# Attention followed by a gated long convolution on one core: another written order for the first two batches, and other transfers for the last rows

## The chip, the cores and the metric

The kernel runs on one core of a Trainium2 chip. The metric is the device time of one execution in microseconds (us). The runs shown of the kernel before have a median of 230.85 us (230.39 to 231.59).

## What is computed

The reference has two halves. A linear attention without softmax, normalised by head, gives `x`; then `x` is projected into three parts, one of them is convolved along the sequence with a filter given in time (576 points, by FFT), multiplied by the two others, and projected out. Batch 8, heads 8, sequence 576, head size 64, so a model size of 512.

```
kv   = einsum('bhsd,bhse->bhde', k, v)
out  = einsum('bhsd,bhde->bhse', q, kv)
attn = out / sqrt(mean(out*out, -1) + 1e-6) * g_norm
x    = attn as [B, S, 512]

x1, x2, x3 = split(x @ w_proj)
X2 = rfft(x2, axis=1);  H = rfft(filter, axis=0)
y  = x1 * irfft(X2 * H) * x3
result = y @ w_out
```

## The kernel before

Everything is written for one core with a schedule made by hand. The body is cut into small named steps, most of them one matmul group on PE (TensorE) or one eviction on ACT (ScalarE) or DVE (VectorE). Three word lists, `FIRST`, `ROUND` and `LAST`, name the steps in the order in which they are issued; a `+` behind a name means one batch later than the round's number, a `-` one batch earlier, and a step that has been issued is not issued again. `FIRST` runs once, `ROUND` for r = 0 to 6, `LAST` once. Each engine works through its own steps in this order, so the lists set the order on PE, ACT, DVE, POOL (GpSimd) and SP (SyncE) alike. Waits between engines follow from the data and the buffers.

The steps of one batch:

- `Lk`, `Lv`, `Lq` (line 98): loads of K, V and Q, 576 KB each in bf16 after a cast from f32, all issued from POOL into one queue, two buffers each (by the batch's parity). For batch 0 K and V come in halves (`Lka`, `Lkb`, `Lva`, `Lvb`). `Lf` loads the filter, `Lw1` to `Lw3` the three thirds of `w_proj`, `Lwo` the output weights.
- `Qt` (line 333): a DMA transpose of Q, issued from SP; batches 0 and 1 use PE instead (`T0`, `T1`, evicted by `eTv` on DVE or `eTa` on ACT).
- `K` (line 307): K transposed times V on PE; `eK` evicts it. For batch 0 in two halves, `Ka` and `Kb`.
- `O0` to `O3` (line 372): attention output for two heads each; `sq` squares it on ACT, `ob` (ACT) or `ov` (DVE, batch 0) scales it by `g_norm`; `R` sums the squares on PE, `rs` takes the reciprocal root on ACT; `x0` and `x1` (line 408, DVE) multiply to `x`.
- `fd`, `fr`, `fa` (DVE): folds of `x` for a transform split by three and by parity. `rrM`, `rrT`, `abM`, `abT` (PE): projection of the folds with the second third of `w_proj`; `err`, `eab`, `eT` (ACT) evict.
- `F0`, `F1`, `F2` (PE): forward transform. `M0`, `M1`, `M2` (DVE): products with the filter's spectrum; `A0` (POOL) and `Av1` (DVE) add them up.
- `Ga0` to `Ga3` and `Gb0` to `Gb3` (line 531, PE): the first and third part of the projection; `x10` to `x13` (ACT) and `g0` to `g3` (DVE) evict and multiply them.
- `Io`, `I` (PE), `os` (ACT), `u`, `w`, `fin` (DVE): inverse transform, unfolding, gate product into `yg`.
- `U0`, `U2`, `U4` (PE, lines 604 and 618): output projection; `ot0`, `ot2`, `ot4` (ACT) evict it and issue the stores, four each, from SP. The last batch uses `V0` to `V3` (one chunk of 128 rows each) with `va` on ACT or `vv` on DVE. `ot_tile` (line 600) hands out three output buffers in turn.

Steps that run once: `Z`, `Zi`, `Zt`, `Zf` (constants), `An0` to `An2` (sine and cosine tables), `Act` (loads ACT's function table for the reciprocal root), `Tb0` to `Tb2` (transposed tables), `Ff0` to `Ff2` (folded filter), `H0` to `H2` (line 269, the filter's spectrum). A step `W..._` adds four matmuls (the first of them ten) without use for the result ahead of the next PE step that takes a PSUM pair (line 78): they keep PE busy.

PSUM is held as four pairs of two banks. A step that writes PSUM takes the pair that was freed longest ago in the written order (line 74), and waits for the step that frees it.

Of the kernel before, what the change touches and what calls it, by code (L numbers as in the profile page):

```python
# [23 lines left out]
Lk++ R1+ x1+ Ga3 Ga2 g1 Io01 rs1+ Gb3 x13 Lv++ x0+ fr+ x12 os01 I01 rrM+ rrT+ fd+ fa+ g3 err+ abT+ eT+ Io23
u01 os23 I23 abM+ F0+ eab+ Gb2 F2+ u23 M0+ F1+ g2 M1+ w23 fin23 w01 fin01 K++ Lk+++ Qt++ Lq+++ eK++ W12_ O2++"""

ROUND = """K++ Lk+++ x0+ Qt++ U0- Lq+++ x13 eK++ fd+ Io23 u01 O2++ fa+ Gb3 fr+ ot0- Lv+++ os23 I23 abM+ g3 sq2++ u23
ob2++ rrM+ eab+ abT+ rrT+ eT+ U4- O1++ w01 err+ ot4- sq1++ ob1++ O3++ sq3++ fin01 ob3++ F1+ U2- w23 fin23 F0+
ot2- M1+ Ga1+ x11+ F2+ Ga0+ M0+ Gb0+ x10+ A0+ R3++ M2+ O0++ Gb1+ g0+ R2++ rs3++ Ga2+ g1+ sq0++ Av1+ ob0++
rs2++ R0++ x1++ Gb2+ x12+ R1++ rs0++ rs1++ g2+ Ga3+ Io01+ os01+ I01+"""  # L30

LAST = """u01 Io23 x13 U0- I23 w01 U2- os23 u23 fin01 ot0- Gb3 w23 ot2- g3 fin23 V2 V1 U4 va2 vv1 V3 V0 ot4 vv3 va0"""


@with_exitstack
def kernel(
# [232 lines left out]
    def gen_h(g):  # L269
        ff = tmp['ff']  # L270
        hp = take("h")
        n = N1 if g == 0 else P
        for ri in range(2):
            for a in range(3):
                m = P if a < 2 else 32
                kw = dict(start=(a == 0), stop=(a == 2))
                if g < 2:
                    nc.tensor.matmul(hp[:n, ri], FW[:m, a, 2 * g + ri, 0:n], ff[:m, a, ri], **kw)
                else:
                    for dup in range(2):  # L280
                        nc.tensor.matmul(hp[dup * NM:(dup + 1) * NM, ri], FW[:m, a, 4 + ri, ri * NM:(ri + 1) * NM], ff[:m, a, ri], **kw)
        u = work.tile([P, 2, DM], FP32, name="hu", tag="ot%d" % g)
        if g < 2:
            todo = [(HH[:n, g, 1], 0, cf[:n, 0, g:g + 1], cf[:n, 1, g:g + 1]),
                    (HH[:n, g, 0], 1, cf[:n, 0, g:g + 1], cf[:n, 2, g:g + 1])]
        else:
            todo = [(HM[:, i], 0, pc[:, 2 * i:2 * i + 1], pc[:, 2 * i + 1:2 * i + 2]) for i in range(2)]
        for i, (o_, ri, c1, c2) in enumerate(todo):
            act.activation(out=u[:n, i], in_=hp[:n, ri], func=AF.Copy, scale=c1)
            vec.scalar_tensor_tensor(out=o_, in0=hp[:n, 1 - ri], scalar=c2, in1=u[:n, i], op0=ALU.mult, op1=ALU.add)  # L290
# [307 lines left out]
    turn = [0]  # L598

    def ot_tile():  # L600
        turn[0] += 1
        return buf("ot", turn[0] % 3, [P, 2, DM], FP32)

# [5 lines left out]
                nc.tensor.matmul(pp[:, cc], ygt(b)[:, dc, c * P:(c + 1) * P], wo[:, dc], start=(dc == 0), stop=(dc == NDC - 1))  # L609

    def U_ev(b, c0):
        ot = ot_tile()
        act.copy(out=ot, in_=tmp['u', b, c0])  # L613
        free(("u", b, c0))
        for i in range(4):
            nc.sync.dma_start(out=o_rows(b, 4 * c0 + i, 4 * c0 + 4 + i), in_=ot[32 * i:32 * i + 32])
# [5 lines left out]
                nc.tensor.matmul(pp[64 * i:64 * i + 64], ygt(b - 1 + i)[:, dc, 4 * P:S], wo[:, dc], start=(dc == 0), stop=(dc == NDC - 1))  # L622

    def U4_ev(b):
        ot = ot_tile()
        act.copy(out=ot[:, 0], in_=tmp['u4', b])
        free(("u4", b))
        for i in range(4):
            nc.sync.dma_start(out=o_rows(b - 1 + i // 2, NB - 2 + i % 2), in_=ot[32 * i:32 * i + 32, 0])

    for c0 in (0, 2):
        step["U%d" % c0] = lambda b, c0=c0: U(b, c0)
# [7 lines left out]
        for dc in range(NDC):  # L640
            nc.tensor.matmul(pp, ygt(b)[:, dc, c * P:(c + 1) * P], wo[:, dc], start=(dc == 0), stop=(dc == NDC - 1))

    def V_ev(b, c, ev, q1):
# [1 line left out]
        ev(out=ot[:, 0], in_=tmp['u', b, c])
        free(("u", b, c))
        for i in range(4):
            (q1 if i >= 2 else nc.sync).dma_start(out=o_rows(b, 4 * c + i), in_=ot[32 * i:32 * i + 32, 0])
# [60 lines left out]
```

## Time and profile before

| what | us |
|---|---|
| median of the runs shown | 230.85 |
| the profiled execution | 231.38 |
| its span on the core | 229.6 |
| PE busy | 209.0 |
| DVE busy | 191.7 |
| ACT busy | 152.3 |

The span is what the profile's times count from and to; the time of the same execution has 1.8 us around it. An engine's busy time counts its own instructions, and matmul ends are modelled, so a busy PE isn't PE at its peak. In a row of the timeline the first number is the start, the second the duration; in brackets stands how long the engine was idle ahead of it and what ended that. A group's row gives, behind the bar, the busy time, the mean of one instruction in ns, and the idle time ahead of them.

### The profile page before, as it was taken

How to read it: one execution, taken by the hardware profiler on the slowest of the kernel's cores; microseconds unless marked ns; L12 is line 12 of the kernel's file. 1: busy time of each engine (PE TensorE's matmuls, PEld its weight loads, DVE VectorE, ACT ScalarE, POOL GpSimd, SP SyncE). 2: the span in 40 equal slices, each digit the busy share in tenths (PEclk: the TensorE clock that was granted, in tenths of full speed). 3: DMA queues.
4: the chain of work that ended last, by engine and by line, in shares of the span. 5: the costliest groups of instructions: out<-in, count | busy, mean ns of one | idle time of the engine just before them, and what ended most of it. 6: DMA issues, size and time to landing. Idle time of an engine off the chain costs nothing.

```text
span 229.6 us, 4731 instructions
## 1 busy us (share of the span) xinstructions
PE 209.0 (91%) x1860; PEld 126.4 (55%) x1881; DVE 191.7 (83%) x323; ACT 152.3 (66%) x238; POOL 45.8 (20%) x55
## 2 busy tenths in 40 slices
PE   7397897899989999999999999999999999999770
PEld 2244433476547755775577557745774676467320
DVE  4864587789898999899889998998899989998920
ACT  7737866995468768776877688768776784533421
POOL 7751000550080000800080008000400040012030
PEclk9859999999999999999999999999999999999995
DMA  4999998599969630999299919993803120350464
GB/s 44 195 202 205 204 207 138 103 142 204 192 100 199 98 91 18 185 184 213 62 185 175 224 34 174 188 206 79 162 3 91 41 55 21 87 126 0 114 179 121
DMA packets 41193, 30.14 MB, mean 131 GB/s; under 512 B 16050, under 2 KB 36530, under 8 KB 41170
## 3 DMA queue, kind: packets, MB, share of 16 engines
q0 software_dynamic: 21200, 17.11, 49.3%
q1 hardware_dynamic: 19778, 12.46, 24.0%
q8 instruction: 15, 0.25, 0.4%
q10 hardware_dynamic: 192, 0.26, 0.4%
q14 instruction: 8, 0.07, 0.1%
HBM read 33.69 MB, written 9.44 MB: 188 GB/s over the span
## 4 chain that ended last, share of the span: by engine, by line
PE 72%; DVE 15%; ACT 6%; issue 2%; DMA 2%; POOL 1%; ACTq 0%; DVEq 0%; POOLq 0%
PE ps L537 26%; PE ps L609 9%; PE ps L464 5%; PE ps L561 4%; PE ps L383 3%; PE ps L471 3%; PE ps L450 3%; PE ps L313 2%; PE ps L376 2%; PE ps L261 2%; PE ps L505 2%; PE ps L497 2%; DMA out_dram<-ot 2%; PE ps L457 1%; PE ps L490 1%
## 5 line engine op out<-in xcount | busy, mean ns | idle before, releaser
L537 PE MATMUL ps<-x,wp 128*128 128x288 bf16 x512 | 71.3, 286 | 0.6 <-ACT o L393 0.5
L537 PEld LDWEIGHTS <-wp 128*128 128x128 bf16 x512 | 49.0, 98 | 17.1 <-issue 1.1
L518 POOL TENSOR_TENSOR Y<-tpw 97x1024 bf16<-97x1024 f32 x8 | 18.8, 2353 | 157.8 <-PE ps L537 79.3
L475 ACT CAST x<-ps 128x1024 bf16<-128x1024 f32 (+1 forms) x24 | 20.3, 871 | 16.3 <-PE ps L464 8.9
L543 ACT CAST x<-ps 128x576 bf16<-128x576 f32 x32 | 20.5, 644 | 12.5 <-PE ps L537 12.0
L545 DVE TENSOR_TENSOR g<-ps,x 128x576 bf16<-128x576 f32 x32 | 24.0, 754 | 5.3 <-PE ps L537 5.1
L609 PE MATMUL ps<-wo,yg 128*128 128x512 bf16 x105 | 26.1, 380 | 0.4
L397 ACT ACTIVATE rstd<-ps,bias_eps 128x576 bf16<-128x576 f32 x32 | 23.6, 745 | 4.2 <-PE ps L383 3.3
L386 ACT ACTIVATE sq<-ps 128x576 bf16<-128x576 f32 x32 | 21.0, 662 | 1.7 <-PE ps L376 1.7
L511 DVE TENSOR_TENSOR tpw<-ps,HH 97x1024 f32<-97x1024 f32 (+1 forms) x16 | 19.5, 1220 | 2.0 <-PE ps L498 1.3
L393 ACT ACTIVATE o<-ps,g_col 128x576 bf16<-128x576 f32 x28 | 21.1, 758 | 0.0
L512 DVE TENSOR_TENSOR tpw<-ps,HH 97x1024 f32<-97x1024 f32 (+1 forms) x16 | 19.4, 1215 | 0.0
L613 ACT COPY ot<-ps 128x1024 f32<-128x1024 f32 x14 | 14.3, 1022 | 7.5 <-PE ps L609 7.4
L609 PEld LDWEIGHTS <-yg 128*128 128x128 bf16 x112 | 10.4, 98 | 11.6
L561 PE MATMUL ps<-IV,Y 128*128 128x192 bf16 x128 | 16.2, 245 | 0.0
L464 PE MATMUL ps<-wp,ab 128*128 128x512 bf16 x64 | 15.1, 379 | 0.0
L565 ACT COPY os<-ps 128x576 f32<-128x576 f32 x16 | 10.3, 642 | 7.1 <-PE ps L562 6.1
L383 PE MATMUL ps<-sq,ind 128*128 128x288 bf16 x64 | 12.9, 286 | 1.9 <-ACT sq L386 1.6
L570 DVE TENSOR_TENSOR u<-ps,os 128x576 bf16<-128x576 f32 x16 | 12.0, 750 | 1.8 <-ACT os L565 1.8
L409 DVE TENSOR_TENSOR x<-o,rstd 128x1152 bf16<-128x1152 bf16 x16 | 12.1, 755 | 1.4 <-ACT rstd L397 1.3
L562 PE MATMUL ps<-IV,Y 97*128 97x96 bf16 x64 | 13.2, 207 | 0.0
L79 PE MATMUL ps<-kvblk,ind 128*128 128x512 bf16 x35 | 11.5, 452 | 1.8 <-DVE ind L145 1.6
(137 smaller groups left out, 339.0 us busy)
## 6 DMA issues: line engine op xcount, KB each, us to landing
out_dram<-ot SPq DMA_DIRECT2D x56, 128.0 KB, 2.4
qb<-in_q_dram POOLq DMA_DIRECT2D x8, 576.0 KB, 9.7
kb<-in_k_dram POOLq DMA_DIRECT2D x7, 576.0 KB, 7.1
vb<-in_v_dram POOLq DMA_DIRECT2D x7, 576.0 KB, 11.7
...
```

The costliest lines, as they stand in the source:

```text
L383: nc.tensor.matmul(r2[:, h, 0:TH], ind, sq()[:, j, h * TH:(h + 1) * TH], start=True, stop=True)
L386: act.activation(out=halves(sq()[:, j]), in_=tmp['o', b, j][:, :, 0:TH], func=AF.Square)
L393: act.activation(out=by_time(osb(), j), in_=i_, func=AF.Copy, scale=g_col)
L397: act.activation(out=by_time(rstd(), j), in_=by_row(tmp['r', b, j]), func=AF.Abs_reciprocal_sqrt, scale=1.0 / D, bias=bias_eps)
L464: nc.tensor.matmul(pp[:, h], abt()[:, j, h * SB:h * SB + P], w2(j), start=(j == 0), stop=(j == NDC - 1))
L475: act.copy(out=o_(), in_=tmp[key, b])
L511: vec.tensor_mul(out=t_[:n, 0], in0=xp[:n], in1=HH[:n, g, 1:3])
L537: nc.tensor.matmul(pp[:, h, 0:TH], w_, x[:, j, h * TH:(h + 1) * TH], start=(j == 0), stop=(j == NDC - 1))
L543: act.copy(out=x1, in_=pp[:, :, 0:TH])
L545: vec.tensor_mul(out=halves(g13t()[:, dc]), in0=pp[:, :, 0:TH], in1=x1)
L561: nc.tensor.matmul(pp[:, i, 0:SB], Y[:, 2 * g + h, cs], IV[:, 2 * g + h, 0:SB], start=(g == 1), stop=(g == 2))
L609: nc.tensor.matmul(pp[:, cc], ygt(b)[:, dc, c * P:(c + 1) * P], wo[:, dc], start=(dc == 0), stop=(dc == NDC - 1))
```

## The change

Three things change.

First, `FIRST` is written anew and is longer: it now reaches to step `I23` of batch 1, and `ROUND` begins at another point of the cycle and has another order inside. For the engines this means:

- Loads are written as Q, then K and V of batch 0 in halves, the filter, Q of batch 1, two thirds of `w_proj`, K of batch 1, the last third, V of batch 1, K, V and Q of batch 2, `w_out`. Before, the filter stood second and the loads of K and V of batch 2 stood behind `A0` of batch 0 on POOL.
- `Act` stands after the sine tables instead of ahead of them.
- The warm-up steps `W6_` to `W9_` and `W12_` are gone; `W0_`, `W1_` and `W2_` stay.
- `Ga0`, `Ga1` of batch 0 stand ahead of K of batch 1, and so on.
- A load into a buffer that a DMA transpose still reads (`Lq++++` after `Qt++`) is written behind the transpose, and in the rounds `Lk`, `Qt`, `A0`, `Lv`, `Lq` follow one another on POOL and SP in another order.

Second, `gen_h` (steps `H0` to `H2`) issues its ACT copies ahead of both DVE products, for g = 0 and 1 as one instruction over both banks.

Third, the last rows. For the last two batches every second output tile is laid into `sq`, `o` or `rstd`, which nothing uses any more, so that six buffers take turns. Two chunks of the last batch share a tile and leave in four transfers of 128 KB (`vd0`, `vd2`, from SP), where each chunk had four of 64 KB from SP and from ACT or POOL. The four transfers of the last `ot4` go from POOL. The order of `LAST` follows.

```diff
-FIRST = """Z Lq Lf Zi Lka Act Zt Lva An0 An1 An2 Lvb W0_ T1 Zf T0 eTv0 eTv1 Tb0 Lkb Lq+ Lw2 Ff2 Ff0 Tb2 Ff1 W2_ Ka eKa W1_ Tb1 O1 sq1
...
+FIRST = """Z Lq Zi W0_ Lvb Zt An0 T1 An2 T0 An1 Lkb Zf eTv0 eTv1 Lka Act W2_ Tb2 Kb eKb Lva Lf Tb1 O3 O2 Ka W1_ sq3 sq2
+eKa R2 R3 Lq+ Lw1 ov2 rs2 ov3 O1 O0 rs3 sq0 ov0 sq1 ov1 Tb0 Lw2 Ff1 Ff0 x1 Lk+ Ff2 R1 R0 Lw3 T1+ rs1 T0+ rs0
+x0 fr0 fr1 eTa1+ eTa0+ H1 fd1 Ga0 Ga1 rrM fa1 x10 x11 fd0 fa0 H2 rrT err H0 abM F0 Lv+ K+ abT Lk++ eK+ O0+ eT
+Lv++ eab Lq++ M0 Gb1 sq0+ ob0+ F1 O1+ sq1+ g1 R0+ Ga3 rs0+ ob1+ M1 F2 O3+ x13 O2+ sq3+ Qt++ sq2+ M2 Av1 ob3+
+Gb3 Lwo Gb0 ob2+ A0 R1+ R2+ g3 R3+ Lq++++ rs1+ g0 x0+ rs2+ rs3+ K++ Io23 x1+ Ga2 eK++ fr+ Io01 x12 O3++ fd+
...
+ROUND = """fd+ fa+ ot0- Ga3 fr+ os23 x13 O2++ I23 sq2++ ob2++ Gb3 abM+ rrM+ g3 abT+ u23 w01 eab+ eT+ rrT+ U4- O1++ O3++
+err+ w23 F1+ ot4- U2- Lk+++ sq1++ sq3++ Qt+++ ob1++ ob3++ F0+ ot2- Ga0+ R3++ fin01 M1+ Ga1+ x10+ rs3++ F2+ M0+
+R1++ A0+ x11+ rs1++ R2++ rs2++ Gb0+ Gb1+ O0++ Av1+ sq0++ M2+ Ga2+ g0+ fin23 ob0++ x12+ Gb2+ Lv++++ Lq+++++
+R0++ g1+ K+++ x1++ Io01+ g2+ I01+ rs0++ U0 os01+ x0++ eK+++ Io23+ u01+"""
-LAST = """u01 Io23 x13 U0- I23 w01 U2- os23 u23 fin01 ot0- Gb3 w23 ot2- g3 fin23 V2 V1 U4 va2 vv1 V3 V0 ot4 vv3 va0"""
+LAST = """I23 w01 os23 u23 Ga3 ot0- fin01 x13 Gb3 w23 U2- ot2- g3 fin23 U4 V3 V2 vv3 ot4 V1 vv1 va2 vd2 V0 va0 vd0"""

+        if g < 2:
+            act.activation(out=u[:n], in_=hp[:n], func=AF.Copy, scale=todo[0][2])
+        else:
+            for i in range(2):
+                act.activation(out=u[:n, i], in_=hp[:n, 0], func=AF.Copy, scale=todo[i][2])
         for i, (o_, ri, c1, c2) in enumerate(todo):
-            act.activation(out=u[:n, i], in_=hp[:n, ri], func=AF.Copy, scale=c1)
             vec.scalar_tensor_tensor(out=o_, in0=hp[:n, 1 - ri], scalar=c2, in1=u[:n, i], op0=ALU.mult, op1=ALU.add)

-    def ot_tile():
+    def ot_tile(b):
+        if b >= B - 2:
+            turn[1] += 1
+            if turn[1] % 2:
+                t = (sq, osb, rstd)[turn[1] // 2 % 3]()
+                return t.rearrange("p a b -> p (a b)").bitcast(FP32)[:, 0:2 * DM].rearrange("p (a b) -> p a b", a=2)
         turn[0] += 1
         return buf("ot", turn[0] % 3, [P, 2, DM], FP32)

-            nc.sync.dma_start(out=o_rows(b - 1 + i // 2, NB - 2 + i % 2), in_=ot[32 * i:32 * i + 32, 0])
+            (nc.gpsimd if b == B - 1 else nc.sync).dma_start(out=o_rows(b - 1 + i // 2, NB - 2 + i % 2), in_=ot[32 * i:32 * i + 32, 0])

-    def V_ev(b, c, ev, q1):
-        ot = ot_tile()
-        ev(out=ot[:, 0], in_=tmp['u', b, c])
+    def V_ev(b, c, ev):
+        if c // 2 not in tmp:
+            tmp[c // 2] = ot_tile(b)
+        ev(out=tmp[c // 2][:, c % 2], in_=tmp['u', b, c])
         free(("u", b, c))
-        for i in range(4):
-            (q1 if i >= 2 else nc.sync).dma_start(out=o_rows(b, 4 * c + i), in_=ot[32 * i:32 * i + 32, 0])
+
+    def V_out(b, c0):
+        for i in range(4):
+            nc.sync.dma_start(out=o_rows(b, 4 * c0 + i, 4 * c0 + 4 + i), in_=tmp[c0 // 2][32 * i:32 * i + 32])
```

More of the change, by code (lines that the diff above doesn't have):

```diff
@@ L24 @@
[L24 to L29, printed above, removed]
@@ new lines @@
+Lv++ eab Lq++ M0 Gb1 sq0+ ob0+ F1 O1+ sq1+ g1 R0+ Ga3 rs0+ ob1+ M1 F2 O3+ x13 O2+ sq3+ Qt++ sq2+ M2 Av1 ob3+
+Gb3 Lwo Gb0 ob2+ A0 R1+ R2+ g3 R3+ Lq++++ rs1+ g0 x0+ rs2+ rs3+ K++ Io23 x1+ Ga2 eK++ fr+ Io01 x12 O3++ fd+
+Lv+++ os01 I01 rrM+ sq3++ ob3++ rrT+ u01 fa+ err+ Gb2 os23 O1++ sq1++ I23 abT+ g2 ob1++ eT+ u23 O2++ w01
+Lv++++ sq2++ Lq+++ O0++ R3++ rs3++ sq0++ ob0++ Lk+++ abM+ F0+ eab+ w23 Ga0+ fin01 ob2++ x10+ F1+ R1++ rs1++
+Ga1+ M0+ x11+ M1+ Gb1+ A0+ R0++ Ga3+ g1+ Qt+++ rs0++ F2+ x13+ Av1+ Gb0+ R2++ rs2++ Ga2+ M2+ g0+ fin23 Io01+
@@ L611, in U_ev @@
     def U_ev(b, c0):
-        ot = ot_tile()
+        ot = ot_tile(b)
         act.copy(out=ot, in_=tmp['u', b, c0])
```

19 lines of the change are left out of this document (9 added, 10 removed).

## The prediction

> **What bounds the kernel now.** I read the head of the page, then a table by stage cut where the path changes hands.
>
> ```profile
> span 229.6 us, 4731 instructions
> PE 209.0 (91%) x1860; PEld 126.4 (55%) x1881; DVE 191.7 (83%) x323; ACT 152.3 (66%) x238; POOL 45.8 (20%) x55
> ```
>
> ```profile
> 0.00:8.83 8.83, 4.45 (x10) 1.31 (x10) 5.47 (x22) 6.12 (x10) 7.38 (x20) 1.00 0.74 97
> 8.83:26.92 18.09, 15.26 (x167) 8.21 (x170) 10.19 (x38) 11.70 (x20) 4.74 (x7) 0.81 1.27 202
> 26.92:40.32 13.40, 11.80 (x74) 4.97 (x75) 10.79 (x24) 8.95 (x13) 0.00 (x0) 1.00 1.08 175
> 40.32:52.31 11.99, 11.07 (x130) 7.10 (x129) 9.15 (x11) 11.65 (x20) 6.16 (x6) 1.00 0.81 129
> 52.31:82.11 29.80, 28.48 (x305) 18.92 (x307) 27.54 (x43) 19.71 (x34) 4.61 (x4) 1.00 0.98 148
> 82.11:104.39 22.28, 22.17 (x212) 14.13 (x212) 21.03 (x32) 16.61 (x27) 4.61 (x4) 1.00 0.75 133
> 104.39:127.54 23.15, 23.05 (x219) 14.57 (x219) 21.21 (x33) 17.21 (x28) 4.63 (x4) 1.00 0.91 159
> 218.27:229.60 11.33, 4.23 (x21) 1.57 (x22) 1.38 (x2) 1.76 (x3) 2.01 (x4) 0.78 0.57 149
> ```
>
> Columns: stretch, length, busy time of PE, PEld, DVE, ACT, POOL, granted clock, DMA share, GB/s. The cuts: 8.83 Q of batch 0 landed; 26.92 first `x` product; 40.32 `M0` of batch 0; 52.31 `x1` of batch 1; 82.11 `abM` of batch 2. From 82.11 on a batch takes 22.28 or 23.15 us, and PE is busy all but 0.1 of it: no order makes these rounds shorter, and DVE has only 1.25 and 1.94 us of room in them. So time can come from three places alone: the fill ahead of 82.11, where DVE was idle 82.11 - (5.47 + 10.19 + 10.79 + 9.15 + 27.54) = 19.0 us; the tail of 11.33 us; and PE stalls that the new round adds. Counting the words of both orders, exactly the same PE steps (warm-ups aside) stand ahead of `abM` of batch 2, so the fill is compared there.
>
> **Fill, loads.** All run in one queue and land in the order written.
>
> ```profile
> 8.83 1.43 PE L340 MATMUL ps<-ident,qb 96*128 96x96 bf16 x24 [2.77 <-DMA qb<-in_q_dram]
> 11.85 0.77 POOL L100 DMA_DIRECT2D vb<-in_v_dram x1 [1.99 <-DMA fn<-in_moe_filter_fft_dram]
> 13.28 0.76 POOL L109 DMA_DIRECT2D wp<-in_moe_w_proj_dram x1 [0.66 <-DMA kb<-in_k_dram]
> 14.72 0.74 POOL L109 DMA_DIRECT2D wp<-in_moe_w_proj_dram x1 [0.67 <-DMA vb<-in_v_dram]
> 16.17 0.74 POOL L109 DMA_DIRECT2D wo<-in_moe_w_out_dram x1 [0.70 <-DMA vb<-in_v_dram]
> 39.99 2.87 SPq L333 DMA_TRANSPOSE qT<-qb  x1
> DMA to landing us min/median/max: 4.8/5.0/7.0
> ```
>
> The ends of these waits are landings: after 576 KB (Q) 8.83, 1152 KB 11.85, then 288 KB every 1.44 us to 16.17 at 2016 KB; the transpose at 39.99 starts when the 14th load (6656 KB in all) is in, so 4640 KB took 23.8 us, 195 KB/us. By this, in the new order: Kb's two halves 11.85, Ka's 14.7 (now the last half lands about 17.6), the filter 17.7 (now 11.85), `wp` thirds 23.2, 25.8 and 31.4, K and V of batch 1 by 34.3, of batch 2 by 40.3, Q of batch 2 at 43.2. The filter and batch 2 pay, attention of batch 0 gains 2.9 us.
>
> **Fill, the chain.** Durations come from these rows:
>
> ```profile
> L397 ACT ACTIVATE rstd<-ps,bias_eps 128x576 bf16<-128x576 f32 x32 | 23.6, 745 | 4.2 <-PE ps L383 3.3
> L386 ACT ACTIVATE sq<-ps 128x576 bf16<-128x576 f32 x32 | 21.0, 662 | 1.7 <-PE ps L376 1.7
> L393 ACT ACTIVATE o<-ps,g_col 128x576 bf16<-128x576 f32 x28 | 21.1, 758 | 0.0
> L263 ACT CAST ff<-ps 128x1024 bf16<-128x1024 f32 x2 | 2.0, 1006 | 2.7 <-PE ps L261 2.7
> L613 ACT COPY ot<-ps 128x1024 f32<-128x1024 f32 x14 | 14.3, 1022 | 7.5 <-PE ps L609 7.4
> 21.91 1.28 ACT L397 ACT_TABLE_LOAD   x1
> 32.33 0.69 ACT L289 ACTIVATE hu<-ps,pc 128x512 f32<-128x512 f32 x1 [1.22 <-DVE HM L290]
> 33.05 0.75 DVE L290 SCALAR_TENSOR_TENSOR HM<-ps,pc,hu 128x512 f32<-128x512 f32 x1 [0.75 <-ACT hu L289]
> ```
>
> First leg, to the first `x0`: ACT works in a row from `sq3` at about 15.1: four `sq`, a `kvblk` pair (0.55), the table copy (0.8), two filter copies, four `rs`: 2.6 + 0.55 + 0.8 + 2.0 + 3.0 = 8.95. The table load of 1.28 that now stands between the first `sq` and its `rs` moves ahead of 13, because `Act` comes after the sines. So x at 24.1, against 26.92: -2.8. Second leg: `H` now takes its two halves in turn, ACT, DVE, ACT, DVE, the ACT copy held 1.22 us by DVE. In the new `gen_h` one ACT copy of 1024 (1.0, as L613) or two of 0.69 run ahead of both DVE products (1.5). DVE has the 10.79 us of the stage 26.92 to 40.32 to do, less one `ov` (0.8, now earlier), and I find 2.0 us of gaps: `M0` starts at 36.1, not 40.32: -4.2. PE has done `Ga0` and `Ga1` by then, two gates of 1 us more than before. Third leg, to `x1` of batch 1: ACT is the path now (11.65 of 11.99 busy) and stays it: less `x10`, `x11` and a copy of H0 that are behind it (1.9), plus `x13` (0.65), 10.4 us, and 1.4 of waits for PSUM pairs: 47.9, -4.4. Fourth leg, to `abM` of batch 2: DVE is the path. Its 27.54 us less one gate product already made (0.7) and less `fr` of batch 2, which now follows `abM` (1.8), plus 1.0 of gaps: 26.1 us, so 74.0, -8.1.
>
> I take two things off. The gaps are those that I could find; the same leg now has 29.80 - 27.54 = 2.3 us of them, so 1.4 more. And `fr` and what follows is owed: DVE enters the round about 2 us later than its place in it, and in the new round adding up PE's and DVE's steps along the new round, the one with least room, `I01`, waits for `g2` with 0.35 us to spare. DVE's room of 1.25 us a round pays part of it: 1.0 us. The fill brings **5.7 us**; from below 2.1 (half of M0's lead survives), from above 8.1 (nothing taken off).
>
> **Warm-ups.** The new order has 18 of the 38 matmuls that only keep PE's clock up.
>
> ```profile
> 1.61 4.45 PE L79 MATMUL ps<-kvblk,ind 128*128 128x512 bf16 x10 [1.61 <-DVE ind L145]
> ...
> L79 PE MATMUL ps<-kvblk,ind 128*128 128x512 bf16 x35 | 11.5, 452 | 1.8 <-DVE ind L145 1.6
> 9.00:10.00 1.00, 1.00 (x24) 1.00 (x22) 0.93 (x4) 0.79 (x3) 0.79 (x1) 0.82 1.14 234
> 16.00:17.00 1.00, 1.00 (x20) 0.76 (x19) 0.00 (x0) 1.00 (x2) 0.74 (x1) 0.77 1.30 199
> 37.58 0.38 PE L488 MATMUL ps<-x,FW 96*97 96x512 bf16 x1 [1.29 <-DVE d__475 L420]
> ```
>
> The clock fell at about 9.6, while PE had had no work from 6.06, and came back at about 16.5 after some 5 us of steady work; a gap of 1.29 us later did not lower it. In the new order steady work begins at 10.3, so full clock at about 15.3, and the gaps that I find after it are under 1.3 us. Removing 20 matmuls that lie in gaps costs nothing by that; the case that it does is a rival. The Trainium skill (TensorE: Matmul & The Clock Gate, Part 1) gives about 3.4 us of sustained activity to release the clock and an idle window of about 3.4 us to lose it. By it full clock would stand at 13.7, and `Kb` and `O3` would end some 0.5 us sooner, though ACT would still wait for Ka; here the first release took some 5 us, so the row is used.
>
> **Rounds.**
>
> ```profile
> 110.03 0.68 ACT L386 ACTIVATE sq<-ps 128x576 bf16<-128x576 f32 x1
> 110.57 0.77 ACT L393 ACTIVATE o<-ps,g_col 128x576 bf16<-128x576 f32 x1
> ...
> 112.32 0.38 PE L488 MATMUL ps<-x,FW 96*97 96x512 bf16 x1
> ```
>
> The new round writes `sq1 sq3 ob1 ob3` where `sq1 ob1 sq3 ob3` stood, so the PSUM pair of `F0` comes free one `sq` (0.54 start to start) later, against 0.98 us of room (111.34 to 112.32) in this round with `U4`, and about 0.4 less in one without (0.86 of PE for `U4`, 0.5 of ACT for its copy): 0.1 us in four of seven rounds, **0.4 us** lost; 0 to 2.5 us as bounds. Keeping transposes apart from loads I price at nothing: a transpose lands after 4.8 to 7.0 us, and now has most of a round until its `O` reads it.
>
> **Tail.**
>
> ```profile
> 217.50 0.76 DVE L582 TENSOR_TENSOR yg<-w,g 128x1152 bf16<-128x1152 bf16 x1
> 219.57 2.73 SPq L648 DMA_DIRECT2D out_dram<-ot  x4
> 222.40 2.77 SPq L629 DMA_DIRECT2D out_dram<-ot  x4
> 223.91 0.58 ACT L645 COPY ot<-ps 128x512 f32<-128x512 f32 x1 [2.51 <-DMA out_dram<-ot]
> 225.27 1.83 SPq L648 DMA_DIRECT2D out_dram<-ot  x4
> ```
>
> From the last `fin23` (218.27) to the end are 11.33 us. ACT's last copy waits 2.51 us for one of three buffers, and SP issues twelve transfers in a row at 0.46 to 0.69 us each until 227.1; the last lands 2.5 us on. After: six buffers, no such wait, `U4`'s four on POOL (done well before), eight on SP. `va2` ends 3.0 us after `fin23`, `va0` 4.65; eight issues at 0.55 end at 7.4, landing at 9.9 to 10: **1.3 us** gained, 0.3 at 0.69 an issue, 2.3 at 0.46. The Trainium skill (DMA: Bandwidth & Descriptors, Issuing engines are not separate DMA queues) says that issuing from several engines saves only the issue time; taking ACT and half of POOL out of it would by this cost SP alone, which the eight issues already count.
>
> **Sum.** 231.38 (the profiled run: 229.6 of span and 1.8 around it) - 5.7 + 0.4 - 1.3 = 224.8. That run was 0.53 above the median of 230.85, so **224.2 us**.
>
> **Rivals.** (a) *Fuller*: the hand chain holds without deductions, tail at its best: 230.85 - 8.1 - 2.3 = 220.4, some 221. For it: ACT's starts lie closer than its durations (sq 0.54 apart). (b) *DVE or the second transpose takes the lead back*: Q of batch 2 lands at 43.2, its transpose at 48.2 to 50.2, and `O3` of batch 2 wants it at 49.2; with 1.0 lost there and the DVE debt paid in full (2.3 more), fill 2.4, tail 1.0, rounds 0.4: 227.9. For it: 43.2 is 3 us later than now. (c) *No change*: the new round stalls 1.0 us each time, 7.0 in seven: 230.9. Against it: the room counted above. (d) *Slower*: with the warm-ups gone the clock stays at half until K of batch 1. PE's busy 15.26 + 11.80 us hold some 20 without warm-ups (11.5 - 4.45), 22 with the two gates, of which 5.5 ran at half clock already; 22 + 16.5 is 38 us from 8.83, K of batch 1 at 46.8 instead of 40.9, 3.9 late after the two gates, tail -1.3: 233.4. It decides if the clock is still 0.50 beyond 25 us. Against it: 16.5 and the 1.29 us gap.
>
> **Chances.** Forecast (223 to 226) 0.45, fuller 0.15, (b) 0.25, (c) 0.07, (d) 0.08. Range 221.0 to 228.6, to leave out (c), (d) and the edge of (a). The measurement tells about 0.5% from no change, 229.7 to 232.0. Faster 0.86, same 0.06, slower 0.08.
>
> **What would show it.** First `x` product near 24, `M0` of batch 0 near 36 to 37, `abM` of batch 2 near 75.5; L289 never waiting for L290; rounds of 22.3 and 23.2; the last `fin23` to the end 10 us. Wrong: a PE wait for `qT`, a clock of 0.50 after 20, rounds above 22.8 and 23.6.

## The result, and the profile after

The changed kernel takes 220.84 us (median of 4 runs, 220.34 to 221.07) where the kernel before, timed beside it, takes 231.04 (230.39 to 231.59): a ratio of 0.956, 95% interval 0.953 to 0.959. The change takes off 10.2 us where 6.6 were forecast, and the time lies 0.16 us below the range's lower end of 221.0. Some executions of the kernel before, and of kernels made from it, run at a lower mean granted clock (0.968 or less) and take 2 to 4 us more, so where that blurs a time in the experiments, a stage is compared instead of the whole.

The head of the page of the changed kernel, and then its stretches, cut at the same steps as before (the first row starts where Q of batch 0 has landed, at 8.46; 23.69 `x0` of batch 0; 35.85 `M0` of batch 0; 47.11 the second `x` product of batch 1; 73.72 `abM` of batch 2; then `abM` of batches 3 and 4; the last two rows are `abM` of batch 7 to the last `fin23`, and from there to the end). Columns: stretch, length, busy time of PE, PEld, DVE, ACT and POOL with instruction counts, granted clock, DMA share, GB/s. Of batch 0's two `x` products, `x0` is the first in the kernel before (26.92, then `x1` at 28.50) and the second in the changed one (`x1` at 21.30, then `x0` at 23.69). Of batch 1's, the second is `x0` in the kernel before (52.31) and `x1` in the changed one.

```profile
span 219.3 us, 4667 instructions
PE 205.3 (94%) x1861; PEld 124.1 (57%) x1861; DVE 191.7 (87%) x323; ACT 148.6 (68%) x234; POOL 50.6 (23%) x55
```

```profile
8.46:23.69 15.23, 14.44 (x187) 8.97 (x188) 11.86 (x40) 12.89 (x23) 6.22 (x9) 1.00 1.24 205
23.69:35.85 12.16, 12.16 (x114) 5.45 (x113) 9.29 (x21) 8.63 (x11) 0.51 (x1) 1.00 1.30 204
35.85:47.11 11.26, 10.45 (x130) 6.51 (x123) 9.83 (x11) 10.72 (x19) 2.36 (x1) 1.00 1.22 178
47.11:73.72 26.61, 24.97 (x244) 16.45 (x242) 26.33 (x42) 18.64 (x32) 7.75 (x8) 1.00 0.94 144
73.72:96.02 22.30, 22.30 (x211) 13.99 (x210) 20.47 (x29) 17.25 (x28) 5.51 (x5) 1.00 1.07 184
96.02:119.19 23.17, 23.17 (x221) 14.45 (x219) 21.27 (x31) 17.13 (x28) 5.44 (x4) 1.00 0.87 160
185.62:208.96 23.34, 22.78 (x161) 13.64 (x158) 23.06 (x37) 9.68 (x13) 3.17 (x1) 1.00 0.32 77
208.96:219.30 10.34, 4.18 (x19) 1.62 (x19) 1.39 (x2) 1.76 (x3) 2.01 (x4) 0.96 0.69 178
```

Three things are to be seen. The rounds are what they were, 22.30 and 23.17 us with PE busy throughout. The fill ends at 73.72 instead of 82.11, and in its last leg DVE is busy 26.33 of 26.61 us: there is next to no gap left in it, where the leg before had 2.3. And the row of the last batch is 23.34 long. The same stretch in the kernel before:

```profile
193.98:218.27 24.29, 22.38 (x157) 13.62 (x156) 22.90 (x37) 9.67 (x13) 2.35 (x1) 1.00 0.34 84
```

| leg, by the two profiled spans | forecast, us | measured, us |
|---|---|---|
| start to `abM` of batch 2 | -5.7 (chain by hand -8.1) | 82.11 to 73.72: -8.39 |
| `abM` of batch 2 to `abM` of batch 7 | +0.4 | 111.9 in both: 0.0 |
| `abM` of batch 7 to the last `fin23` | 0 | 24.29 to 23.34: -0.95 |
| last `fin23` to the end | -1.3 | 11.33 to 10.34: -0.99 |
| sum | -6.6 | 229.6 to 219.3: -10.3 |

Within the fill, the stretches that end at `x0`, at `M0`, at the second `x` product of batch 1 and at `abM` of batch 2 bring -3.23, -1.24, -0.73 and -3.19.

One new wait stands in the fill. The chain of waits of the changed kernel, followed back from 74 us (start, length, what):

```profile
42.88 5.66 DMA qT<-qb
...
52.24 15.50 DMA kb<-in_k_dram
67.74 0.04 issue
67.79 0.95 PE ps L321 x48
```

And POOL's loads in its timeline (start, length, what; in brackets the idle time ahead and what ended it), with PE's largest waits between 8 and 74 us (us in total, times, longest):

```profile
49.13 0.82 POOL L104 DMA_DIRECT2D qb<-in_q_dram  x1 [8.48 <-DMA qT<-qb]
49.95 1.53 POOL L104 DMA_DIRECT2D vb<-in_v_dram  x2
51.48 0.77 POOL L104 DMA_DIRECT2D qb<-in_q_dram  x1
52.24 0.77 POOL L104 DMA_DIRECT2D kb<-in_k_dram  x1
```

```profile
PE ps L348 <- DMA qb<-in_q_dram: 2.4, 1, 2.4
PE ps L321 <- DMA kb<-in_k_dram: 1.1, 1, 1.1
```

The first load behind the transpose `Qt` of batch 2 waits 8.48 us on POOL for it, it and four more then go out in a row, and K of batch 3, the fifth, lands 15.50 us after its issue, 1.1 us after PE wants it. There is no PE wait for `qT`, so the transpose itself is in time.

### The profile page after: what moved, and what is told of

The parts are those of the page before. It is cut to its first block, busy times and chain, and to the rows that moved or that the text cites. A ratio compares the mean times of both kernels' runs of the same rounds, so it can differ in the third digit from the quotient of the medians.

```text
span 219.3 us, 4667 instructions
## 1 busy us (share of the span) xinstructions
PE 205.3 (94%) x1861; PEld 124.1 (57%) x1861; DVE 191.7 (87%) x323; ACT 148.6 (68%) x234; POOL 50.6 (23%) x55
## 4 chain that ended last, share of the span: by engine, by line
PE 74%; DMA 13%; DVE 4%; ACT 3%; issue 1%; POOL 1%; POOLq 0%; ACTq 0%
PE ps L545 23%; PE ps L622 10%; DMA kb<-in_k_dram 7%; PE ps L472 6%; PE ps L569 4%; DMA qb<-in_q_dram 3%; PE ps L321 3%; PE ps L458 3%; PE ps L479 3%; DMA qT<-qb 3%; PE ps L391 2%; PE ps L513 2%; PE ps L384 2%; PE ps L654 2%; PE ps L505 2%; PE ps L282 2%
## 5 line engine op out<-in xcount | busy, mean ns | idle before, releaser
L545 PE MATMUL ps<-x,wp 128*128 128x288 bf16 x512 | 70.4, 286 | 0.3 <-ACT x L483 0.3
L526 POOL TENSOR_TENSOR Y<-tpw 97x1024 bf16<-97x1024 f32 x8 | 23.4, 2924 | 122.8 <-DVE tpw L520 85.6
L405 ACT ACTIVATE rstd<-ps,bias_eps 128x576 bf16<-128x576 f32 x32 | 22.8, 740 | 6.1 <-PE ps L391 6.0
L394 ACT ACTIVATE sq<-ps 128x576 bf16<-128x576 f32 x32 | 20.3, 664 | 6.2 <-PE ps L384 5.9
L401 ACT ACTIVATE o<-ps,g_col 128x576 bf16<-128x576 f32 x28 | 20.4, 759 | 0.0
L626 ACT COPY ot<-ps 128x1024 f32<-128x1024 f32 x13 | 13.3, 1021 | 8.9 <-PE ps L622 8.9
L573 ACT COPY os<-ps 128x576 f32<-128x576 f32 x16 | 10.3, 641 | 6.5 <-PE ps L570 6.5
L590 DVE TENSOR_TENSOR yg<-w,g 128x1152 bf16<-128x1152 bf16 x16 | 14.2, 886 | 0.0
L391 PE MATMUL ps<-sq,ind 128*128 128x288 bf16 x64 | 11.9, 286 | 0.3 <-ACT x L483 0.3
```

The costliest lines, as they stand in the source:

```text
L394: act.activation(out=halves(sq()[:, j]), in_=tmp['o', b, j][:, :, 0:TH], func=AF.Square)
L401: act.activation(out=by_time(osb(), j), in_=i_, func=AF.Copy, scale=g_col)
L405: act.activation(out=by_time(rstd(), j), in_=by_row(tmp['r', b, j]), func=AF.Abs_reciprocal_sqrt, scale=1.0 / D, bias=bias_eps)
L526: op(out=Yt()[:n, 2 * g:2 * g + 2], in0=t_[:n, :, 0], in1=t_[:n, :, 1])
L545: nc.tensor.matmul(pp[:, h, 0:TH], w_, x[:, j, h * TH:(h + 1) * TH], start=(j == 0), stop=(j == NDC - 1))
```

## The experiments

The head differs between executions: `x0` of batch 0 lies between 22.84 and 24.06 in all kernels with the changed kernel's head (the landing of Q of batch 0, at 8.2 in one trace and 8.4 in another of the changed kernel, makes up only a part). Stages are therefore counted from `x0`. In the changed kernel `M0` of batch 0 comes 12.16 and `abM` of batch 2 50.03 us after it.

### The loads behind the transpose

K of batch 3 as third of the five loads:

```diff
-O3++ fd+ Lv+++ os01
+O3++ fd+ Lv+++ Lk+++ os01
...
-ob0++ Lk+++ abM+
+ob0++ abM+
```

> The changed kernel with the load of K of batch 3 moved from last of five to third behind the transpose of Q of batch 2. In the changed kernel K of batch 3 starts 1.13 us after PE is free, at the landing of that load (67.74). Theory A (the load queue behind the transpose ends the fill): that wait goes, abM of batch 2 comes near 72.6 instead of 73.72, time 219.8 against 220.84 (1.0 faster). Theory B (the DVE debt I took off in the prediction is real and shows once the wait is gone): abM comes at 73.4 or later because fa or fr isn't done, time within 0.3 of 220.84.

Measured: 220.26 us (219.74 to 220.61), ratio 0.947 (0.942 to 0.953). The wait for K is gone, `abM` of batch 2 comes 49.35 us after `x0`, and the rounds stay at 22.30 and 23.17. So a fill that ends 0.7 us earlier is not paid back in the rounds: the "DVE debt" of the prediction does not exist at this size. One PE wait of 0.6 us for a transpose (`O2` of batch 3, for `qT`) takes its place.

With the loads shared out over both transposes (Q of batch 4, V, K and Q of batch 3 behind the first; V of batch 4 behind the second):

```diff
-O3++ fd+ Lv+++ os01
+O3++ fd+ Lv+++ Lk+++ Lq+++ os01
...
-w01 Lv++++ sq2++ Lq+++ O0++
+w01 sq2++ O0++
...
-ob0++ Lk+++ abM+
+ob0++ abM+
...
-K+++ Lq+++++ os01+
+K+++ Lq+++++ Lv++++ os01+
```

> The changed kernel with the loads behind the first transpose in the order Q of batch 4, V, K and Q of batch 3, and V of batch 4 written behind the second transpose. In the run with K of batch 3 third, abM of batch 2 came at 72.34 and the only wait left ahead of it was 0.61 us of O2 of batch 3 for the second transpose. Theory A: that wait goes too, from abM of batch 1 to abM of batch 2 are 17.4 us instead of 17.92 (18.59 as changed), time 219.6 to 220.0. Rival: the second transpose meets another load and lands as late, time 220.3 as before or above.

Measured: 220.41 us (220.15 to 221.28), ratio 0.951 (0.945 to 0.956). PE has no wait for a load or a transpose left between 38 and 80 us, and `abM` of batch 2 comes 48.82 us after `x0`, 1.2 sooner than in the changed kernel. DVE is as full in that leg as before (25.17 of 25.41 us), with three instructions fewer in it, so a full DVE doesn't show that DVE bounds the leg. Neither time can be told from that of the changed kernel itself, run once more:

> The changed kernel itself once more, to stand beside the two that follow. A time of 220.4 to 221.2 us; the head up to the first full x product may lie some 1 us elsewhere than 23.69, since the landing of Q differs from run to run, and the steps counted from there should be the same: M0 of batch 0 12.2 us after it, abM of batch 2 50.0 us after it, abM of batch 7 to the end of the last fin23 23.34, from there to the end 10.34.

Measured: 220.45 us (219.8 to 220.93), ratio 0.951 (0.946 to 0.956); `M0` 12.16, `abM` of batch 2 50.20 after `x0`, then 23.34 and 10.32.

### The loads beside the transpose

The same loads ahead of the one that waits for the transpose, so that they are under way when it is issued:

```diff
-R3+ Lq++++ rs1+
+R3+ Lv+++ Lk+++ Lq+++ Lq++++ rs1+
...
-fd+ Lv+++ os01
+fd+ os01
...
-sq2++ Lq+++ O0++
+sq2++ O0++
...
-ob0++ Lk+++ abM+
+ob0++ abM+
```

> The changed kernel with the loads of V, K and Q of batch 3 written ahead of the load that waits for the transpose, so that they run beside it (from 40.7 instead of 49.1). If a transpose is hurt by loads beside it: it lands at 51 or later instead of 48.5, O3 of batch 2 (now at 48.67) waits for it by 2 us or more, time 221.5 or above. If loads and the transpose only share bandwidth: the transpose lands by 49.5, K of batch 3 no longer waits, time as in the run with the loads behind, 219.8.

Measured: 231.31 us (230.56 to 233.02), ratio 0.997 (0.993 to 1.001). The whole gain is lost. PE's wait in this kernel, POOL's loads, and two stretches of 4 us with the columns of the first table:

```profile
PE ps L384 <- DMA qT<-qb: 10.0, 1, 10.0
```

```profile
40.02 0.82 POOL L104 DMA_DIRECT2D vb<-in_v_dram  x1
40.84 0.77 POOL L104 DMA_DIRECT2D kb<-in_k_dram  x1
41.60 0.77 POOL L104 DMA_DIRECT2D qb<-in_q_dram  x1
59.20 0.77 POOL L104 DMA_DIRECT2D qb<-in_q_dram  x1 [16.83 <-DMA qT<-qb]
```

```profile
52.00:56.00 4.00, 0.00 (x0) 0.00 (x0) 0.00 (x0) 0.00 (x0) 0.00 (x0) 0.62 1.30 171
56.00:60.00 4.00, 1.22 (x11) 0.97 (x12) 0.00 (x0) 0.66 (x2) 0.80 (x2) 0.50 0.73 65
```

From 52 to 56 no engine does anything while the DMA engines are busy with the loads and the transpose (DMA share 1.30); `O3` of batch 2 waits 10.0 us for its Q, and the clock falls to 0.50 meanwhile. From `abM` of batch 0 to that of batch 1 it takes 34.88 us instead of 22.64. A dose of one load in place of three:

```diff
-R3+ Lq++++ rs1+
+R3+ Lv+++ Lq++++ rs1+
...
-fd+ Lv+++ os01
+fd+ os01
```

> The changed kernel, but V of batch 3 is loaded ahead of the load that waits for the first transpose (so beside that transpose) instead of behind it: one load of 576 KB beside the transpose where an earlier run had three. Theory (a transpose gets hardly any of the DMA engines while a load is queued, and lands when the load is through): one load of 576 KB at about 195 KB per us is 3.0 us, so the transpose lands 3 us later, at about 51.5, and O3 of batch 2 waits for it some 2 us; the K wait behind it goes or shrinks, so the time rises by 0.5 to 2.0 us, far less than with three loads (10.5). Rival (the cost is a fixed one of mixing the two kinds, whatever the amount): a PE wait for qT of 8 us or more and a time of 228 to 232. Second rival (the prediction's: a transpose beside loads costs nothing): no PE wait for qT and a time within 0.5 of the changed kernel.

Measured: 223.39 us (221.63 to 224.28), ratio 0.961 (0.955 to 0.967), 2.9 us above the changed kernel timed beside it:

```profile
PE ps L384 <- DMA qT<-qb: 3.6, 1, 3.6
```

```profile
40.13 0.82 POOL L104 DMA_DIRECT2D vb<-in_v_dram  x1
52.31 0.77 POOL L104 DMA_DIRECT2D qb<-in_q_dram  x1 [11.35 <-DMA qT<-qb]
```

The load held back by the transpose goes out at 52.3 instead of 49.1. From its issue to its landing the transpose takes 5.66 us in the changed kernel, 8.84 with one load more beside it and 14.85 with three (a load of `w_out`, which lands at 46.2 to 46.7, runs beside it in all three). That is 3.2 and 9.2 us more, where one and three loads of 576 KB at the 195 KB/us of the prediction take 3.0 and 8.9. So the transpose comes through after the loads, and the cost is not a fixed one. It doesn't follow that it gets nothing meanwhile: the three loads land at 50.2, 54.4 and 58.1, some 4 us apart, where loads without a transpose beside them land 2.9 apart (V and Q of batch 2 at 39.87 and 42.79 in the changed kernel), and the transpose lands at 58.65. Both are slowed. The size of the wait was set too low (2), because `O3` of batch 2 has hardly any room there: in the changed kernel the transpose lands at 48.54 and `O3` starts at 48.67. Two of the six executions with one load took 221.6 to 221.7, so the cost differs between them.

### The filter's place, `gen_h`, the table

The filter second in the load queue again, as before the change:

```diff
-Z Lq Zi W0_ Lvb
+Z Lq Lf Zi W0_ Lvb
...
-eKb Lva Lf Tb1
+eKb Lva Tb1
```

> The changed kernel with the filter's load back in second place, ahead of K and V of batch 0, everything else as changed. K and V of batch 0 land 2.9 us later, the filter earlier. Theory A: first x product near 25.5 to 26.5 instead of 23.69, part of that is taken up by the 1.13 us wait: time 221.8 to 222.8. If the load order is what the fill's gain is made of: 223.7 (the whole 2.9).

Measured: 223.43 us (223.19 to 223.74), ratio 0.961 (0.956 to 0.967). `x0` comes at 26.96, where the kernel before had 26.92, and `M0` 12.16 us after it. But these are different products in the order of batch 0: the first in the kernel before, the second here. The second of the kernel before, the first of the changed kernel, and the second of this one:

```profile
28.50 0.76 DVE L409 TENSOR_TENSOR x<-o,rstd 128x1152 bf16<-128x1152 bf16 x1
```

```profile
21.30 0.75 DVE L417 TENSOR_TENSOR x<-o,rstd 128x1152 bf16<-128x1152 bf16 x1
```

```profile
26.96 0.76 DVE L417 TENSOR_TENSOR x<-o,rstd 128x1152 bf16<-128x1152 bf16 x1 [0.53 <-ACT rstd L405]
```

The second product comes 4.8 us earlier in the changed kernel (28.50 to 23.69). With the filter second again 3.3 of it are lost; the other 1.5 stay and come from the rest of the new order. A part of the 3.3 may be the clock's, which is 0.51 from 10 to 20.4 us in this trace and 1.00 in that of the changed kernel; no run separates the two, and the head's own spread (22.84 to 24.06) stands beside all these differences. At `abM` of batch 2 2.06 us are left (75.78 against 73.72), because K of batch 3 then no longer comes late: no PE wait for a load is left there.

`gen_h` as before, in the changed kernel:

```diff
-        if g < 2:
-            act.activation(out=u[:n], in_=hp[:n], func=AF.Copy, scale=todo[0][2])
...
         for i, (o_, ri, c1, c2) in enumerate(todo):
+            act.activation(out=u[:n, i], in_=hp[:n, ri], func=AF.Copy, scale=c1)
```

> The changed kernel with the old gen_h (ACT and DVE in turn). Theory A: M0 of batch 0 comes 1.5 to 2 us later than 35.85, but K of batch 3 waits for its load by 1.13 us anyway and takes that much of it: time 221.3 to 221.8 (0.5 to 1.0 slower). Theory C (the chain through ACT and DVE alone sets the fill): the whole 1.5 to 2 us shows, 222.3 to 222.8.

Measured: 220.95 us (220.53 to 221.67), ratio 0.951 (0.945 to 0.956). `M0` comes 13.90 us after `x0` instead of 12.16, so the new `gen_h` is worth 1.74 us at that place; at `abM` of batch 2 0.28 are left of it (50.31 after `x0`), and the time doesn't show it. What comes out of the second leg earlier waits for K of batch 3.

`Act` ahead of the tables again:

```diff
-Lvb Zt An0
+Lvb Act Zt An0
...
-Lka Act W2_
+Lka W2_
```

> The changed kernel with the word Act ahead of the sine tables again, so that ACT reloads the sine table and loads the other table a second time between sq and the first rs (1.28 us each). Theory A: the fill's chain runs through ACT there, M0 of batch 0 comes some 1.2 later, and the 1.13 us wait of K of batch 3 takes nearly all of it: 220.9 to 221.4. If ACT has room there: M0 as before the edit, 220.8.

Measured: 221.56 us (220.34 to 222.93), ratio 0.955 (0.949 to 0.961). ACT's first rows of the reciprocal root in this kernel:

```profile
16.27 1.28 ACT L405 ACT_TABLE_LOAD   x1
17.56 1.37 ACT L405 ACTIVATE rstd<-ps,bias_eps 128x576 bf16<-128x576 f32 x2
```

The table load stands between `sq` and `rs` again, and yet `rs` starts at 17.56, where the kernel with the loads shared out, whose `x0` lies at the same 24.06, has it at 17.57 behind a wait of 0.47 us for PE. So in this trace ACT has room there, and `Act`'s place brings nothing. The trace is of an execution of 220.8; three of the six took 222.2 to 222.9, and what took longer in those is not shown.

### The warm-ups

The kernel before without its 20 warm-up matmuls that the change leaves out:

```diff
-R0 rs0 W6_ R1
+R0 rs0 R1
...
-ov2 W7_ O3
+ov2 O3
...
-fa1 W8_ H1 F0 W9_ abM
+fa1 H1 F0 abM
...
-eK++ W12_ O2++
+eK++ O2++
```

> The kernel before without the warm-ups W6 to W9 and W12 (20 matmuls without use), nothing else changed. The prediction's step: they lie in gaps and the clock does not fall without them, so the first full x product stays within 0.5 us of 26.92, M0 of batch 0 within 1 us of 40.32, the time within 0.7 us of the kernel before or up to 1 us below it. Rival (the prediction's slower case: without them the clock stays at half until K of batch 1): granted clock of 0.50 in rows after 20 us, M0 of batch 0 2 to 4 us later, time 2 to 4 us above the kernel before.

Measured: 234.35 us (233.74 to 236.74), ratio 1.014 (1.007 to 1.020). The rival held. Two stretches in this kernel, then the second of them in the kernel before (in the changed one PE is busy 13.34 us of it, at 1.00):

```profile
21.40:24.60 3.20, 1.22 (x28) 0.97 (x29) 2.47 (x8) 3.15 (x5) 0.00 (x0) 0.98 1.30 203
24.00:38.00 14.00, 12.37 (x59) 4.85 (x62) 8.41 (x17) 9.04 (x14) 0.00 (x0) 0.52 1.27 204
```

```profile
24.00:38.00 14.00, 11.66 (x77) 4.74 (x79) 10.97 (x24) 10.38 (x16) 0.00 (x0) 1.00 1.27 204
```

Without the warm-ups the clock is 0.52 from 24 to 38 us, and `M0` of batch 0 comes 16.1 us after `x0` (43.30) instead of 13.4 (40.32). At `abM` of batch 2, 57.8 after `x0` instead of 55.2, 2.6 us are lost. PE's timeline in this kernel, just ahead of the fall at about 24.5:

```profile
22.57 0.65 PE L383 MATMUL ps<-sq,ind 128*128 128x288 bf16 x4 [1.17 <-ACT sq L386]
23.36 0.57 PE L313 MATMUL ps<-vb,kb 96*64 96x64 bf16 x24
24.62 0.39 PE L376 MATMUL ps<-qT,kvblk 64*64 64x288 bf16 x1 [0.69 <-ACT rstd L397]
```

The longest gap is 1.17 us, shorter than the 1.29 us that the prediction took as harmless; but PE is busy only 1.22 of 3.20 us. The Trainium skill (TensorE: Matmul & The Clock Gate, Part 1) has the clock fall after an idle window of about 3.4 us; here there is no such uninterrupted stretch, and the clock falls with PE 38% busy over 3.2 us. In the changed kernel PE is busy 2.99 of the same 3.20 us, and the clock is 1.00 through the fill of its trace.

But neither the longest gap nor this share tells by itself when the clock falls. The kernel before has PE idle for 2.77 us ahead of 8.83, and its clock falls at 9.6. The kernel before with `Ga3` late, used further down, has the same first batches and the same gap (2.78 us), with PE busy 0.42 of 3.20, and in its trace the clock stays at 1.00:

```profile
5.80:9.00 3.20, 0.42 (x4) 0.15 (x4) 2.99 (x9) 2.03 (x5) 3.18 (x5) 1.00 1.23 199
```

And behind the gap of 1.29 us, after which the kernel before kept its clock, the clock does fall in the trace of the kernel before with `Av1` early, which has all the warm-ups:

```profile
38.70 0.38 PE L488 MATMUL ps<-x,FW 96*97 96x512 bf16 x1 [1.29 <-DVE d__475 L420]
```

```profile
39.20:42.80 3.60, 3.60 (x11) 1.29 (x10) 2.85 (x5) 1.36 (x3) 0.00 (x0) 0.53 0.44 82
```

`abM` of batch 2 then comes 56.9 us after `x0`, 1.7 later than in the kernel before and 0.95 sooner than without the warm-ups. What decides between these traces is open.

### The tail

The old tail (three buffers, a transfer of its own for each chunk) in the changed kernel:

```diff
-fin23 U4 V3 V2 vv3 ot4 V1 vv1 va2 vd2 V0 va0 vd0
+fin23 V2 V1 U4 va2 vv1 V3 V0 ot4 vv3 va0
```

> The changed kernel with the old output tiles, the old V steps and their old order behind the last fin23. If the new tail brings what the spans from the last fin23 to the end show (11.33 against 10.34): 1.0 slower, 221.8. If that difference is due to what runs ahead of the tail and not to the tail's own edit: within 0.3 of 220.84.

Measured: 221.93 us (221.66 to 222.72), ratio 0.957 (0.952 to 0.962); from the last `fin23` to the end 11.28 us. The tail's edit is worth 11.28 - 10.34 = 0.94 us. SP's last issues in the changed kernel:

```profile
212.11 1.73 SPq L664 DMA_DIRECT2D out_dram<-o  x4
213.95 2.33 SPq L664 DMA_DIRECT2D out_dram<-rstd  x4
```

The last issue ends at 216.28, 7.32 us after the last `fin23` (7.4 in the prediction), but the last transfer lands 3.02 us on, at 219.30, not 2.5.

### The last batch

The 0.95 us between `abM` of batch 7 and the last `fin23` were not foreseen. DVE is the path there. Its timeline in the kernel before, and in the changed one:

```profile
205.60 1.22 DVE L527 TENSOR_TENSOR Y<-ps,HM 128x1024 bf16<-128x1024 f32 x1
206.73 1.42 DVE L545 TENSOR_TENSOR g<-ps,x 128x576 bf16<-128x576 f32 x2
208.06 1.23 DVE L518 TENSOR_TENSOR Y<-tpw 128x1024 bf16<-128x1024 f32 x1
209.22 0.74 DVE L545 TENSOR_TENSOR g<-ps,x 128x576 bf16<-128x576 f32 x1
211.00 0.76 DVE L570 TENSOR_TENSOR u<-ps,os 128x576 bf16<-128x576 f32 x1 [1.04 <-ACT os L565]
```

```profile
196.41 1.22 DVE L526 TENSOR_TENSOR Y<-tpw 128x1024 bf16<-128x1024 f32 x1
197.54 1.22 DVE L535 TENSOR_TENSOR Y<-ps,HM 128x1024 bf16<-128x1024 f32 x1
198.67 0.75 DVE L553 TENSOR_TENSOR g<-ps,x 128x576 bf16<-128x576 f32 x1
199.34 1.11 DVE L590 TENSOR_TENSOR yg<-w,g 128x1152 bf16<-128x1152 bf16 x1
200.37 1.41 DVE L553 TENSOR_TENSOR g<-ps,x 128x576 bf16<-128x576 f32 x2
201.70 0.74 DVE L578 TENSOR_TENSOR u<-ps,os 128x576 bf16<-128x576 f32 x1
```

In the kernel before, DVE waits 1.04 us for `os`; in the changed one it waits for nothing. Of what differs ahead of that wait, three things were tried: `Ga3` of batch 7 stands in `LAST` behind the inverse transform, `fin23` of batch 6 (the `yg` row) stands later, and the sum `Av1` (the row `Y<-tpw`) stands ahead of the gate products. Each was moved alone, and two together, in the last round only. In the kernel before, `Ga3` late (with `Ga3` then standing behind `u23` in `LAST`):

```diff
-        do(ROUND, r)
+        do(ROUND if r < B - 2 else ROUND.replace("Ga3+ ", ""), r)
...
-LAST = """u01 Io23 x13 U0- I23 w01 U2- os23 u23 fin01
+LAST = """u01 Io23 U0- I23 w01 os23 u23 Ga3 ot0- fin01 x13 Gb3 w23 U2-
```

> The kernel before with one thing changed: Ga3 of the last batch, written ahead of its Io01 and I01, goes behind I23, as the changed kernel has it, with x13 and U2 following. Theory: the last batch ends on the chain I01, os23, u, w, fin on DVE, so a gate of 1 us ahead of I01 is paid in full: last fin23 0.9 earlier, 0.9 faster than before (ratio 0.996). Rival: DVE is what the end waits for and is full there anyway, so nothing moves: ratio within 0.999 to 1.001.

In the changed kernel, `fin23` of batch 6 early:

```diff
-        do(ROUND, r)
+        do(ROUND if r < B - 2 else ROUND.replace("fin01 M1+", "fin01 fin23 M1+"), r)
```

> The changed kernel, but in the last round alone fin23 of batch 6 stands right behind fin01 of batch 6, as in the kernel before, and no longer behind Av1 of batch 7. Open is where the 0.94 us between abM of batch 7 and the end of the last fin23 come from. Theory (a wait filled): DVE is the path in this stage; in the kernel before it waits 1.04 us for the eviction os of batch 7, and in the changed kernel the 0.7 to 1.1 us of this fin23 lie in that place. Then DVE waits 0.7 to 1.0 us for os again, the stage grows from 23.34 to 24.0 to 24.3, and the time is 0.7 to 0.9 us above that of the changed kernel in the same job. Rival (the order of Ga3 and of the Y sums, which also differs, makes os early): the stage stays within 0.2 us of 23.34 and DVE waits for nothing.

In the kernel before, `Av1` early:

```diff
-        do(ROUND, r)
+        do(ROUND if r < B - 2 else ROUND.replace("R3++ M2+", "R3++ Av1+ M2+"), r)
```

> The kernel before, but in the last round alone Av1 of batch 7 (DVE's sum of products, 1.2 us) stands ahead of M2 and of g0 and g1, as in the changed kernel, instead of behind them. Theory (the sum's place): the inverse transform of batch 7 waits for both sums; with Av1 early it starts while DVE still makes gate products, so os is ready when DVE comes to it. Then DVE no longer waits 1.04 us for os, the stage from abM of batch 7 to the end of the last fin23 falls from 24.28 to 23.4 or less, and the time by 0.7 to 1.0 us. Rival (the transform starts when PE has done its gates, Ga3 among them, whatever the sums do): the stage stays at 24.1 to 24.3, DVE waits some 1.0 us.

In the changed kernel, `Av1` late:

```diff
-        do(ROUND, r)
+        do(ROUND if r < B - 2 else ROUND.replace("Av1+ ", "").replace("g1+ K+++", "g1+ Av1+ K+++"), r)
```

> The changed kernel, but in the last round alone Av1 of batch 7 stands behind g0 and g1 on DVE, as in the kernel before. Theory (the sum's place): the stage from abM of batch 7 to the end of the last fin23 grows from 23.34 to 24.0 to 24.4, with a DVE wait of 0.7 to 1.1 us for os. Rival: the stage stays within 0.2 us of 23.34.

In the kernel before, the first and the third of these edits together:

> The kernel before, last round and LAST alone: Ga3 of batch 7 late (as in an earlier run, which gained 0.35 us in the stage, with PE then waiting 0.45 us for the sum of Av1) and Av1 ahead of M2 (as in another, which gained nothing, with Ga3 then keeping PE until 1.1 us after the sums). Theory (the inverse transform waits for whichever of the two is later, so only both together bring it forward): the transform starts some 1.0 us sooner, DVE waits 0.3 us or less for os, and the stage from abM of batch 7 to the end of the last fin23 is 23.2 to 23.6 against 24.28. Rival (each has its own small effect and they add up): the stage is 23.9 or more and DVE waits 0.6 us or more.

The stage and the wait are read from the profiled execution; the granted clock is 1.00 in that stage in each.

| kernel | time, us | `abM` of batch 7 to last `fin23` | DVE waits for `os` |
|---|---|---|---|
| kernel before | 231.04 | 24.29 | 1.04 |
| before, `Ga3` late | 231.69 (230.84 to 234.96), ratio 0.999 (0.995 to 1.003) | 23.93 | 0.69 |
| before, `Av1` early | 232.96 (230.93 to 234.23), ratio 1.002 (0.997 to 1.007) | 24.54 | 1.12 |
| before, both | 233.29 (230.34 to 234.4), ratio 1.001 (0.995 to 1.006) | 23.55 | none |
| changed kernel | 220.84 | 23.34 | none |
| changed, `fin23` early | 220.80 (220.46 to 221.66), ratio 0.953 (0.948 to 0.958) | 23.35 | none |
| changed, `Av1` late | 221.83 (221.6 to 222.68), ratio 0.956 (0.951 to 0.961) | 24.47 | 0.7 |

The theory of a wait filled by `fin23` fell: moved back, it changes nothing. The theory of the sum's place held in the changed kernel, where `Av1` late brings the wait back and costs 1.13 us, and fell for `Av1` alone in the kernel before. With `Av1` late PE waits 1.0 us for the sum. The inverse transform needs both: DVE's sum, and PE free of `Ga3`. With `Ga3` late alone, PE waits for the sum:

```profile
PE ps L561 <- DVE Y L518: 0.5, 1, 0.5
```

With both, DVE's wait is gone and the stage is 23.55 long, 0.74 of the 0.95 us; what the remaining 0.2 are is open. The total times of the three kernels made from the kernel before say nothing on so small a matter: they lie between 230.3 and 235.0.

## Why the prediction was right or wrong

**The sign was right, and so was most of the mechanism; the size was 3.7 us short** by the profiled executions (224.8 against 221.07), and the nearest case was the rival *Fuller* (220.4, chance 0.15). That this one comes so close is luck in part: it has the tail at -2.3, measured -0.99, and nothing for the last batch, measured -0.95.

- *The chain by hand of the fill* was right nearly step by step: `x0` at 23.69 (24.1), `M0` at 35.85 (36.1), `x1` of batch 1 at 47.11 (47.9), `abM` of batch 2 at 73.72 (74.0), each as measured and, in brackets, as predicted. Not every term was: the last leg was put together from 25.1 us of DVE's work and 1.0 of gaps, and holds 26.33 and 0.28. Nor does the first leg's "24.1, against 26.92" compare like with like: 24.1 is the end of both products, 26.92 the first of two, so that gain is 4.8 us and not 2.8. By the experiments, the filter's place in the queue carries 3.3 of it; the table load, which the prediction credited with 1.28, has no part in the trace. No run isolates the third and the last leg's gain (0.73 and 3.19 us), which the new order as a whole brings; there the cause is the chain's argument alone.
- *"I take two things off"* is the step that failed, 2.4 of the 3.7 us: the fill brought 8.39 us, the chain without deductions said 8.1, and with them 5.7. The 1.4 us of further gaps were taken from a leg of another order. In the last leg DVE stands idle 26.61 - 26.33 = 0.28 us, and even that leg still holds a PE wait of 1.1 for K of batch 3, which the chain had not. The 1.0 us of "DVE debt" isn't there: the rounds keep 22.30 and 23.17 whether the fill ends at 72.34 or 75.78.
- *Rounds, +0.4*: measured 0.0. `F0`'s pair of PSUM, freed one `sq` later, costs nothing; PE is busy all of the round.
- *"Time can come from three places alone"* was wrong: there is a fourth, the last batch, where PE has fewer steps and DVE is the path. The prediction looked at the rounds alone, where PE is the path. 0.95 us.
- *The tail, -1.3*: -0.99, and 0.94 by the old tail in the changed kernel. The issues ended when forecast; the landing behind the last one was sized at 2.5 us and took 3.0.
- *Warm-ups at nothing*: the number was right, the reason was not. "A gap of 1.29 us later did not lower it" doesn't make gaps under 1.3 us safe: taken out of the old order, the same matmuls cost 3.3 us by the medians and 2.6 in the traces' fill, and the clock did fall behind that same gap in another trace. That they cost nothing in the new order because the real work fills their place is argued from PE's 2.99 of 3.20 us; no run puts them back there. The rival *Slower* had the mechanism right, in the wrong kernel.
- *Transposes apart from loads, "at nothing"*: in the changed kernel no PE wait for `qT` shows, as forecast. But it is nothing because they are kept apart: the 4.8 to 7.0 us of the prediction were read off transposes with little beside them (4.80 with no load left, 7.01 with one that landed 3.1 us after the transpose's issue). With three loads beside it the change would have given 231.31, no gain at all. The rival (b), a second transpose that takes the lead back, named this place, but looked for the cause in Q's own landing. The Trainium skill (DMA: Bandwidth & Descriptors, Rules for kernel authors) says "A transpose next to ordinary DMAs needs nothing"; that stands beside rules on corrupted data, and for the time the runs here say otherwise: a wait of 3.6 us for one load of 576 KB, 10.0 for three.
